# Where the last 64 rows of Wv stand among the first weight loads of a recurrent transformer kernel

## The chip, the cores and the metric

The kernel runs on one core of one Trainium2 chip. The metric is device time in microseconds (us) from one launch, the median of several runs. Everything is bf16 with fp32 sums in PSUM.

## The reference

Two blocks are applied twice, each as `x = x + block(layernorm(x))`, over a sequence of 2048 tokens of width 576. The first block is attention with a recurrent memory: the sequence is cut into 64 segments of 32 tokens, each is preceded by 8 memory tokens, and the first 8 output tokens of a segment are the memory of the next. The second is a gated feed-forward of width 4608.

```python
for s in range(n_seg):
    xs = x[:, s * seg_len:(s + 1) * seg_len, :].copy()
    h = jnp.concatenate([mem, xs], axis=1)
    q = jnp.einsum('btd,dhe->bhte', h, Wq)
    k = jnp.einsum('btd,dhe->bhte', h, Wk)
    v = jnp.einsum('btd,dhe->bhte', h, Wv)
    scores = jnp.einsum('bhqe,bhke->bhqk', q, k) * scale
    scores = jnp.where(mask[None, None], scores, -1000000000.0)
    p = _softmax(scores, axis=-1)
    o = jnp.einsum('bhqk,bhke->bhqe', p, v)
    o = jnp.einsum('bhte,hed->btd', o, Wo)
    mem = o[:, :M, :].copy()
    outs.append(o[:, M:, :])
# feed-forward: silu(x @ w1) * (x @ w3) @ w2
```

There are 32 heads of 128, so Wq, Wk and Wv are 576 x 4096 each and Wo is 4096 x 576.

## The kernel before

The segments are a chain of 72 steps: in step t the first attention block does segment t and the second one segment t - 8, and feed-forward work fills the gaps between. Which matmul comes when on PE is a string of letters (`ORDER`) written out by hand. A planner gives every other engine its order from costs, priorities and buffers. SP issues most transfers, ACT four at the start and one at the end. WARM adds plain matmuls at named places, so that PE has something to do there.

The width of 576 is not a multiple of 128: every weight with 576 rows is four blocks of 128 rows and a tail of 64. The tails of Wq and Wk lie side by side in one buffer, `W[:, 8, :]`, each over 64 partitions, 4096 columns. The tail of Wv is 64 rows of 4096 columns as well, but its buffer, the last 2048 columns of `WV`, spreads it over all 128 partitions: columns are cut into 8 pieces of 512, and piece 2q + r lies in the 64 partitions r of columns 512 q and on (q from 0 to 3, r 0 or 1).

All weights of the attention are loaded in one burst at the start. In the order of the program these are, as the text calls them:

- ACT: the tail of Wk, the first 128 tokens (`XN`), the memory (`XTB`, 8 rows), and the half r = 1 of the Wv tail;
- SP: the tail of Wq, the half r = 0 of the Wv tail, then the first halves of the columns of Wq and Wk (four transfers each of 128 rows, 0.5 MB apiece, `load_qk(0)`), their second halves (`load_qk(1)`), the four blocks of Wv (1 MB apiece, `load_v`), the four parts of Wo by groups of 8 heads (`load_o`), and then the first feed-forward weights.

Each transfer takes one of eight semaphores in turn (`DMAHW0` to `DMAHW7`), and its issue waits until the transfer before it on that semaphore has landed. So at most eight are under way.

On PE the first step is: transposes of the first tokens, warm matmuls that read Wk (three for each block, each waiting for its block), Q and K of the first four quarters of the heads (`QK`, `QKt` is its tail part), one group of scores, 22 warm matmuls, Q and K of the other heads, softmax work between, then V. For t = 0 V begins with its tail (16 matmuls of 64 rows, letters `vx`), followed by the four blocks in turn (64 matmuls, letter `X`), a block for all banks at a time. Then come the product with the probabilities (`PV`) and the output projection by groups of 8 heads (`WO`, 32 matmuls and 8 for its tail columns); group g reads part g of Wo.

Of the kernel before, what the change touches and what calls it, by code (L numbers as in the profile page):

```python
# [9 lines left out]
ACT = mybir.ActivationFunctionType  # L10
# [3 lines left out]
P = 128  # L14
R64 = 64
D = 576
# [10 lines left out]
NG = 4  # L27
# [215 lines left out]
def make_nodes(em, nseg, pools, o=Opt, dma_bw=230e3, load_bw=400e3):  # L243
# [4 lines left out]
    def node(*a, **k):  # L248
        n = Node(*a, **k)
        nodes.append(n)  # L250
        return n
# [5 lines left out]
    kb = lambda rows, cols: rows * cols * 2  # L257
# [9 lines left out]
    def load(name, nbytes, prio, fn, deps=()):  # L267
        return node("DMA", nbytes / load_bw, fn, deps=deps, prio=prio, name=name, lat=2.0)

    node("DMA", 4.0, lambda n: None, prio=-999.0, name="boot")  # L270
    ld_m0 = node("ACT", 0.6, em.load_m0(), prio=-90, name="m0", lat=8.0)
    ld_t = [load("ldt", 1.7 * kb(3 * R64, 4096), -10.0, em.load_tails(0)), node("ACT", 0.6, em.load_tails(1), prio=-120, name="ldt", lat=8.0)]
    node("ACT", 0.6, em.load_tails(2), prio=-80, name="ldt", lat=10.0)
    ld_h = [load("ldqk", kb(512, 4096), half - 9.0, em.load_qk(half)) for half in (0, 1)]
    ld_v = [load("ldv", kb(512, 4096), -7.0, em.load_v())]
    ld_o = [load("ldo", kb(1024, 576), g - 6.0, em.load_o(g)) for g in range(NG)]

    b = banks(1)
# [349 lines left out]
class Emitter:  # L628
# [110 lines left out]
        return f  # L739

    def load_tails(self, what):
        def f(n):
            if what < 2:
                d, wd = (self.dma, self.a.wq) if what == 0 else (self.adma, self.a.wk)
                d(self.T.W[what * R64:(what + 1) * R64, 8, :], wd[4 * P:D, :])
            if what != 1:
                r = what // 2
                (self.adma if r else self.dma)(self.wv(True)[r * R64:(r + 1) * R64, :].rearrange("p (q n) -> p q n", q=NG),
                                               self.a.wv[4 * P:D, :].rearrange("p (q r n) -> r p q n", q=NG, r=2)[r])
        return f  # L750

    def wv(self, tail):
        if tail:
# [2 lines left out]

    def load_v(self):
        def f(n):
            for c in range(4):
                self.dma(self.wv(False)[:, c, :], self.a.wv[c * P:(c + 1) * P, :])  # L760
        return f
# [555 lines left out]
def kernel(  # L1317
# [26 lines left out]
    em = Emitter(nc, tc, T, a, nseg)  # L1344
    pools = dict(POOLS)
    nodes = make_nodes(em, nseg, pools)

    wp = ctx.enter_context(tc.tile_pool(name="wts", bufs=1))
# [97 lines left out]
```

## Time and profile before

| | |
|---|---|
| median of 3 runs | 2624.2 us (2623.95 to 2626.34) |
| profiled execution | 2624.02 us |
| its span, first to last instruction | 2622.2 us |
| PE busy | 98% |
| DVE, ACT, POOL busy | 77%, 48%, 7% |
| bytes moved | 369.58 MB, 141 GB/s over the span |
| first fortieth of the span (65.6 us) | PE 60%, 326 GB/s |
| granted TensorE clock | 0.999 |

The profile is of one execution. All times in it count from the first instruction. A row of a timeline gives start, duration, engine, line, operation and the tiles written and read; lines with "DMA" on SPq or ACTq are issues of transfers, whose duration is the issue alone. "DMA to landing" is the time from issue until the data have arrived. L653, L672 and L675 are the helpers that record every matmul, every transfer of SP and every transfer of ACT, so one goes by tiles.

### The profile page before, as it was taken

What the parts mean: (1) busy time and instruction counts of PE and PEld (TensorE: products, weight loads), DVE (VectorE), ACT (ScalarE), POOL (GpSimd) and SP (SyncE); (2) the same over time, 40 slices, a digit from 0 to 9 for tenths busy, and PEclk for the clock granted to TensorE, in tenths of its full rate; (3) what the DMA queues carried; (4) which work ended last, traced back from release to release, by engine and by line L of the source; (5) the groups of instructions that cost most, each with busy time, mean ns of one, the idle gap of its engine ahead of it and who ended that gap; (6) DMA issues with size and microseconds to landing.
All of it is one profiled execution on the core that took longest, in us unless ns stands there. A gap on an engine that the chain in (4) does not pass through costs nothing.

```text
span 2622.2 us, 131462 instructions
## 1 busy us (share of the span) xinstructions
PE 2567.1 (98%) x58447; PEld 2205.6 (84%) x58498; DVE 2009.5 (77%) x5145; ACT 1266.8 (48%) x3743; POOL 196.1 (7%) x253
## 2 busy tenths in 40 slices
PE   6999999999999999999999999999999999999998
PEld 4788888888888888888888888888888888888887
DVE  4778777787787688777867877786787778777877
ACT  2655453544545354454535445453544545445553
POOL 1100000000001000000000000010000000010000
PEclk9999999999999999999999999999999999999999
DMA  9064746565464656555465655546465554554447
GB/s 326 4 181 126 193 103 154 126 152 136 126 139 115 148 128 153 135 126 141 115 148 128 155 133 127 144 109 151 128 156 132 126 143 112 128 146 129 123 131 258
DMA packets 680217, 369.58 MB, mean 141 GB/s; under 512 B 233592, under 2 KB 669824, under 8 KB 679008
## 3 DMA queue, kind: packets, MB, share of 16 engines
q1 hardware_dynamic: 675968, 353.23, 52.5%
q8 instruction: 457, 7.49, 1.2%
q0 software_dynamic: 3024, 6.93, 0.9%
q10 hardware_dynamic: 656, 1.02, 0.2%
q14 instruction: 112, 0.92, 0.1%
HBM read 304.95 MB, written 2.36 MB: 117 GB/s over the span
## 4 chain that ended last, share of the span: by engine, by line
PE 90%; DMA 4%; DVE 3%; SPq 1%; issue 1%; ACT 1%; ACTq 0%; DVEq 0%
PE bank L653 90%; DMA PTS<-PB 2%; DMA W<-in_B_w_dram 1%; SPq L672 1%; DVE STAT L669 1%; DVE PB L669 1%; DVE SME L669 1%; DMA WV<-in_A_Wv_dram 0%; DVE HTT L669 0%; DMA W<-in_A_Wk_dram 0%; ACT V L666 0%; DVE V L669 0%; PE bank L663 0%; DMA W2C<-in_B_w_dram 0%; ACT HT L666 0%
## 5 line engine op out<-in xcount | busy, mean ns | idle before, releaser
L653 PEld LDWEIGHTS <-W 128*128 128x128 bf16 (+2 forms) x32096 | 1252.3, 100 | 121.3 <-issue 66.1
L653 PE MATMUL bank<-HT,W 128*128 128x80 bf16 (+3 forms) x23040 | 792.9, 197 | 9.6 <-ACT HT L666 5.4
L653 PE MATMUL bank<-XTB,W 128*64 128x256 bf16 (+5 forms) x9056 | 662.5, 264 | 4.5 <-DMA W<-in_B_w_dram 4.2
L666 ACT ACTIVATE QKT<-bank 128x192 bf16<-128x192 f32 (+4 forms) x1674 | 382.2, 312 | 274.5 <-PE bank L653 268.7
L653 PE MATMUL bank<-OT,WO 128*128 128x80 bf16 (+3 forms) x11520 | 411.1, 198 | 1.3 <-issue 1.3
L653 PEld LDWEIGHTS <-WO 128*128 128x128 bf16 (+1 forms) x11520 | 380.4, 102 | 27.6 <-issue 13.4
L666 ACT ACTIVATE V<-bank 64x512 bf16<-64x512 f32 (+1 forms) x589 | 333.0, 585 | 136.7 <-PE bank L653 129.8
L653 PE MATMUL bank<-WV,HT 128*32 128x512 bf16 (+4 forms) x3430 | 355.9, 381 | 6.8 <-issue 4.3
L653 PE MATMUL bank<-W2C,HTT 128*64 128x288 bf16 (+1 forms) x3152 | 322.1, 287 | 0.7 <-DMA W2C<-in_B_w_dram 0.6
L666 ACT ACTIVATE HTT<-bank 128x512 bf16<-128x512 f32 (+1 forms) x324 | 173.1, 550 | 284.0 <-PE bank L653 283.1
L669 DVE SCALAR_TENSOR_TENSOR XR<-bank,XR 128x288 f32<-128x288 f32 x574 | 243.4, 448 | 59.0 <-PE bank L653 53.4
L669 DVE TENSOR_REDUCE STAT<-SME 104x8 f32<-104x320 f32 (+1 forms) x576 | 273.8, 475 | 12.2 <-ACT SME L666 5.0
L669 DVE TENSOR_TENSOR PB<-SME,STAT 40x128 bf16<-40x128 f32 (+4 forms) x912 | 275.1, 336 | 8.1 <-issue 0.2
L653 PEld LDWEIGHTS <-HT 128*32 128x32 bf16 (+4 forms) x3472 | 147.5, 98 | 140.3 <-issue 24.9
L1092 POOL MEMSET PB<- 128x1024 bf16 x142 | 134.8, 951 | 1742.7 <-DMA PTS<-PB 1219.4
L653 PEld LDWEIGHTS <-HTT 128*64 128x64 bf16 (+1 forms) x3232 | 231.4, 105 | 35.7 <-issue 5.6
L669 DVE SCALAR_TENSOR_TENSOR HTT<-HTT,bank 128x512 bf16<-128x512 bf16 (+1 forms) x324 | 200.9, 620 | 69.7 <-ACT HTT L666 65.8
L666 ACT ACTIVATE OT<-bank 128x320 bf16<-128x320 f32 (+1 forms) x389 | 145.1, 402 | 203.8 <-PE bank L653 196.6
L669 DVE TENSOR_TENSOR HTT<-HTT,bank 128x512 bf16<-128x512 bf16 (+1 forms) x324 | 203.5, 628 | 28.0 <-DVE HTT L669 0.9
L666 ACT ACTIVATE SME<-SME 104x320 f32<-104x320 f32 (+1 forms) x288 | 135.0, 469 | 180.9 <-DVE SME L669 179.0
L669 DVE CAST V<-bank 64x512 bf16<-64x512 f32 (+1 forms) x275 | 188.3, 685 | 40.8 <-PE bank L653 36.4
L669 DVE TENSOR_TENSOR SME<-bank,maskb 104x320 f32<-104x320 f32 (+1 forms) x288 | 138.9, 483 | 39.4 <-PE bank L653 36.1
(61 smaller groups left out, 1400.8 us busy)
## 6 DMA issues: line engine op xcount, KB each, us to landing
W<-in_B_w_dram SPq DMA_DIRECT2D x604, 256.0 KB, 3.5
W2C<-in_B_w_dram SPq DMA_DIRECT2D x302, 288.0 KB, 3.5
W<-in_B_w_dram SPq DMA_DIRECT2D x604, 32.0 KB, 3.5
W<-in_B_w_dram SPq DMA_DIRECT2D x8, 1024.0 KB, 13.0
W<-in_A_Wq_dram SPq DMA_DIRECT2D x9, 512.0 KB, 9.9
WO<-in_A_Wo_dram SPq DMA_DIRECT2D x4, 1152.0 KB, 16.8
XR<-in_A_x_dram POOLq DMA_DIRECT2D x16, 288.0 KB, 2.9
WV<-in_B_w_dram SPq DMA_DIRECT2D x4, 1152.0 KB, 12.3
```

Source lines behind the costliest of these rows:

```text
L653: self.ch("PE", self.nc.tensor.matmul(out, lhsT=lhsT, rhs=rhs, start=start, stop=stop, skip_group_check=True, **k))
L666: self.ch("ACT", self.nc.scalar.activation(*a, **k))
L669: self.ch("DVE", getattr(self.nc.vector, fn_)(*a, **k))
L672: self.ch("SP", self.nc.sync.dma_start(out=out, in_=in_))
L1092: return lambda n: self.ch("POOL", self.nc.gpsimd.memset(self.pbt(pb), 0.0))
```

## The change

The two transfers of the Wv tail are gone from the head of ACT's and SP's queues. In their place four stand on SP behind the second halves of Wq and Wk, ahead of the blocks of Wv. Each fills 512 columns of all 128 partitions; its source is a view of Wv with r (2) outermost, then the 64 rows, then 512 columns.

```diff
-    ld_t = [load("ldt", 1.7 * kb(3 * R64, 4096), -10.0, em.load_tails(0)), node("ACT", 0.6, em.load_tails(1), prio=-120, name="ldt", lat=8.0)]
-    node("ACT", 0.6, em.load_tails(2), prio=-80, name="ldt", lat=10.0)
+    ld_t = [load("ldt", 1.7 * kb(2 * R64, 4096), -10.0, em.load_tails(0)), node("ACT", 0.6, em.load_tails(1), prio=-120, name="ldt", lat=8.0)]
     ld_h = [load("ldqk", kb(512, 4096), half - 9.0, em.load_qk(half)) for half in (0, 1)]
-    ld_v = [load("ldv", kb(512, 4096), -7.0, em.load_v())]
+    ld_v = [load("ldv", kb(576, 4096), -7.0, em.load_v())]
...
     def load_tails(self, what):
-        def f(n):
-            if what < 2:
-                d, wd = (self.dma, self.a.wq) if what == 0 else (self.adma, self.a.wk)
-                d(self.T.W[what * R64:(what + 1) * R64, 8, :], wd[4 * P:D, :])
-            if what != 1:
-                r = what // 2
-                (self.adma if r else self.dma)(self.wv(True)[r * R64:(r + 1) * R64, :].rearrange("p (q n) -> p q n", q=NG),
-                                               self.a.wv[4 * P:D, :].rearrange("p (q r n) -> r p q n", q=NG, r=2)[r])
-        return f
+        d, wd = (self.dma, self.a.wq) if what == 0 else (self.adma, self.a.wk)
+        return lambda n: d(self.T.W[what * R64:(what + 1) * R64, 8, :], wd[4 * P:D, :])
...
     def load_v(self):
         def f(n):
+            for q in range(NG):
+                self.dma(self.wv(True)[:, q * 512:(q + 1) * 512], self.a.wv[4 * P:D, q * 1024:(q + 1) * 1024].rearrange("p (r n) -> r p n", r=2))
             for c in range(4):
                 self.dma(self.wv(False)[:, c, :], self.a.wv[c * P:(c + 1) * P, :])
         return f
```

SP at the start of the program, before the change; the brackets name the semaphore of the earlier transfer for whose landing the issue waits:

```order
L672 DMA W<-in_A_Wq_dram 64x4096
L672 DMA WV<-in_A_Wv_dram 64x4x512
L672 DMA W<-in_A_Wq_dram 128x2048 x2
L672 DMA W<-in_A_Wq_dram 128x2048 [waits DMAHW0_49]
L672 DMA W<-in_A_Wq_dram 128x2048 [waits DMAHW1_49]
L672 DMA W<-in_A_Wk_dram 128x2048 [waits DMAHW2_49]
L672 DMA W<-in_A_Wk_dram 128x2048 [waits DMAHW3_49]
L672 DMA W<-in_A_Wk_dram 128x2048 [waits DMAHW4_49]
```

And with the change, at the same place:

```order
L671 DMA W<-in_A_Wq_dram 64x4096
L671 DMA W<-in_A_Wq_dram 128x2048 x4
L671 DMA W<-in_A_Wk_dram 128x2048 [waits DMAHW0_49]
L671 DMA W<-in_A_Wk_dram 128x2048 [waits DMAHW1_49]
L671 DMA W<-in_A_Wk_dram 128x2048 [waits DMAHW2_49]
L671 DMA W<-in_A_Wk_dram 128x2048 [waits DMAHW3_49]
```

The transfer of the Wv tail has left SP's head, and all four blocks of Wq are issued there without a wait. The four blocks of Wk now wait for the tail of Wk, the tail of Wq, the first tokens and the first block of Wq, and no more for the two halves of the Wv tail.

SP further on, with the change, from the last block of Wk's second half to the first blocks of Wv; the first dimension of a row is that of the destination's partitions:

```order
L671 DMA W<-in_A_Wk_dram 128x2048 [waits DMAHW3_49]
L671 DMA WV<-in_A_Wv_dram 128x1x512 [waits DMAHW4_49]
L671 DMA WV<-in_A_Wv_dram 128x1x512 [waits DMAHW5_49]
L671 DMA WV<-in_A_Wv_dram 128x1x512 [waits DMAHW6_49]
L671 DMA WV<-in_A_Wv_dram 128x1x512 [waits DMAHW7_49]
L671 DMA WV<-in_A_Wv_dram 128x4096 [waits DMAHW0_49]
L671 DMA WV<-in_A_Wv_dram 128x4096 [waits DMAHW1_49]
```

Before, the row of the last Wk block is followed at once by those of the Wv blocks. The four tail transfers stand ahead of all of Wv and, with it, of Wo and the feed-forward weights.

PE at the start of V in step 0 (the last warm matmul, and the first of the 16 tail matmuls), before:

```order
L663 MATMUL bank_88<-W,ident 128x512
L653 LDWEIGHTS HT
L653 MATMUL bank_88<-WV,HT 32x512
L653 LDWEIGHTS HT
L653 MATMUL bank_88<-WV,HT 32x512
```

And with the change:

```order
L652 LDWEIGHTS HT
L652 MATMUL bank_88<-WV,HT 32x512 [waits DMAHW4_49]
L652 LDWEIGHTS HT
L652 MATMUL bank_88<-WV,HT 32x512 [waits DMAHW5_49]
L652 LDWEIGHTS HT
L652 MATMUL bank_88<-WV,HT 32x512 [waits DMAHW6_49]
L652 LDWEIGHTS HT
L652 MATMUL bank_88<-WV,HT 32x512 [waits DMAHW7_49]
```

Nothing has moved on PE, but the first four tail matmuls now wait for one of the four transfers each. On PE, DVE, ACT and POOL the order of all operations is as before over the whole program (ACT has one issue less), and so is that of the transfers on SP behind the blocks of Wv.

## The prediction

> **What bounds the kernel now.** I read the page first, then the chain of waits of the first 90 us, then DMA and clock in stretches of 2 us, and last the transfers one by one. The chain over the whole span:
>
> ```profile
> PE 90%; DMA 4%; DVE 3%; SPq 1%; issue 1%; ACT 1%; ACTq 0%; DVEq 0%
> ```
>
> PE carries the kernel. The edit touches only the loads of the first 60 us, and the order of the work on PE, DVE and ACT stays the same, so what it does there is added to, or taken from, the end almost one to one. The chain there begins with the very transfers that are moved:
>
> ```profile
> 2.86 11.15 DMA WV<-in_A_Wv_dram
> 14.02 0.02 issue
> 14.03 8.94 DMA W<-in_A_Wk_dram
> 22.97 0.04 issue
> 23.01 5.11 PE bank L653 x170
> ```
>
> ACT's half of the Wv tail lands at 14.02; only then does SP issue the last block of Wk's first half, which lands at 22.97 and starts Q and K. What limits this stage is DMA, as the stretches show (length; PE, PEld, DVE, ACT, POOL; then granted clock, DMA share, GB/s):
>
> ```profile
> 6.00:8.00 2.00, 0.00 (x0) 0.00 (x0) 1.78 (x5) 0.00 (x0) 0.00 (x0) 1.00 0.98 196
> 8.00:10.00 2.00, 0.00 (x0) 0.00 (x0) 0.45 (x1) 0.00 (x0) 0.00 (x0) 1.00 1.09 295
> 10.00:12.00 2.00, 0.00 (x0) 0.00 (x0) 1.18 (x4) 0.00 (x0) 0.56 (x1) 1.00 1.02 321
> 12.00:14.00 2.00, 0.94 (x10) 0.76 (x11) 1.08 (x5) 0.68 (x1) 0.01 (x1) 1.00 1.06 354
> 18.00:20.00 2.00, 2.00 (x6) 0.67 (x5) 0.00 (x0) 0.00 (x0) 0.00 (x0) 1.00 1.07 406
> 44.00:46.00 2.00, 0.82 (x20) 0.20 (x5) 1.78 (x5) 0.67 (x2) 0.00 (x0) 1.00 1.09 390
> 46.00:48.00 2.00, 1.82 (x36) 1.05 (x39) 0.13 (x1) 0.00 (x0) 0.00 (x0) 1.00 1.08 385
> ```
>
> The engines of DMA are full (share about 1) while the Wv tail is under way, yet move only 196 to 354 GB/s; with nothing but Wq and Wk blocks it is 406, and with Wo, whose rows are 1152 bytes, 385 to 390. From here on a transfer lands when all before it in the queue are through.
>
> **The head of the queue.** Removed: two transfers of 256 KB, 0.52 MB together, ahead of Wk's last block. At 406 GB/s that is 1.3 us, at 196 it is 2.7; I take the mean rate of the three stretches from 8 to 14 us, 323 GB/s, so 1.6 us. Second, a wait goes:
>
> ```profile
> 10.03 4.33 SPq L672 DMA_DIRECT2D W<-in_A_Wk_dram  x4
> 24.27 4.16 SPq L672 DMA_DIRECT2D WV<-in_A_Wv_dram  x4
> 29.38 16.75 SPq L672 DMA_DIRECT2D WO<-in_A_Wo_dram  x4
> ```
> ```profile
> SPq L672 <- DMA WV<-in_A_Wv_dram: 2.7, 1, 2.7
> ```
>
> The four Wv issues wait for the four second-half blocks of Wq in turn, so their spacing is that of landings: 4.16 less an issue of 0.33 is 3.83 for three, 1.28 us a block. The fourth Wk block was issued at 14.03, after 2.7 us of waiting. Had it been issued at once, it could have landed up to 2.7 us sooner; if the queue was long enough to hide that, 0 sooner. I take 1.6, a little over one block's spacing, since the engines were full all the while. Gain at the head: 3.2 us, between 1.3 and 5.4. So Q and K would begin at 19.8. Two more rows matter here, the first tokens on their way into HT, and the landing of Wk's last block (issue near 23.0, then 10.2):
>
> ```profile
> 14.61 0.96 ACT L666 ACTIVATE HT<-bank 128x320 bf16<-128x320 bf16 x4
> ```
> ```profile
> L672 SPq DMA_DIRECT2D W<-in_A_Wk_dram x1: 328/328/328, 23.0 to 23.0; - x1
> DMA to landing us min/median/max: 10.2/10.2/10.2
> ```
>
> The tokens are there by 15.6 and are not late. Wk's last block landed at 33.2 and comes 3.2 us sooner as well, at 30.0, so PE keeps the whole gain until V.
>
> **What the four new transfers cost.** They carry the same 0.52 MB. The question is how many of the 16 DMA engines carry it. The source view has r = 2 outermost, the destination 128 partitions. No transfer before has an outermost step so small, but one is near it: the memory, 8 rows. ACT's queue holds these transfers and no others:
>
> ```profile
> q10 hardware_dynamic: 656, 1.02, 0.2%
> ```
> ```profile
> W<-in_A_Wk_dram ACTq DMA_DIRECT2D x1, 512.0 KB, 7.6
> WV<-in_A_Wv_dram ACTq DMA_DIRECT2D x1, 256.0 KB, 11.2
> XN<-in_A_x_dram ACTq DMA_DIRECT2D x1, 144.0 KB, 8.7
> out_dram<-XN ACTq DMA_DIRECT2D x1, 72.0 KB, 1.6
> XTB<-in_A_mem_dram ACTq DMA_DIRECT2D x1, 9.0 KB
> ```
>
> Their contiguous rows are 64 + 256 + 128 + 128 + 8 = 584. The queue has 656 packets, 72 more: 4 x 16 + 8. So four transfers end with one packet on each of 16 engines, and the one of 8 rows with 8: a transfer seems to be dealt out in equal parts along its outermost step. A number of engines that cuts both sides evenly, 2 of the source and 128 of the destination, is 2. I take that as the likeliest: each transfer of 128 KB runs on two engines, 64 KB on each, and all four on the same two.
>
> [...]
>
> The price: four times 64 KB is 262 KB on each of the two. An engine moves a sixteenth of the stretches' rate. Bounds: with 406 GB/s (25.4 per engine) 10.3 us; with Wo's small rows at 390 (24.4) 10.7; with 1 KB rows beside other loads at 321 (20.1) 13.1; at 196 (12.3) 21.4. These are 1 KB rows beside other loads as in the stretch from 10 to 12, so I take 13.1.
>
> Who waits for that: all that stands behind the tails on SP goes over all engines, thus also over these two, and lands 13.1 - 3.2 = 9.9 us later than before. The landings before, the last block of Wv and the last part of Wo:
>
> ```profile
> L672 SPq DMA_DIRECT2D WV<-in_A_Wv_dram x1: 328/328/328, 28.1 to 28.1; - x1
> DMA to landing us min/median/max: 15.1/15.1/15.1
> ...
> L672 SPq DMA_DIRECT2D WO<-in_A_Wo_dram x1: 2898/2898/2898, 43.2 to 43.2; - x1
> DMA to landing us min/median/max: 11.8/11.8/11.8
> ```
>
> That is 43.2 and 55.0; with the change 53.1 and 64.9. And their readers on PE:
>
> ```profile
> 43.79 0.63 PE L653 MATMUL bank<-WV,HT 64*32 64x512 bf16 x16
> 46.18 3.42 PE L653 MATMUL bank<-WV,HT 128*32 128x512 bf16 x60 [0.90 <-DVE V L669]
> 55.14 3.21 PE L653 MATMUL bank<-OT,WO 128*128 128x40 bf16 x116
> ```
>
> V ended at 49.6 with its last block's matmuls, a quarter of 3.42, 0.86 us. Now that block lands at 53.1 and V ends at 54.0, 4.4 us late. The 116 rows of WO are 32 of group 1, 32 of group 2, 16 for tail columns, 32 of group 3 and 4 more, so group 3 began at about 55.14 + 80/116 x 3.21 = 57.4, 2.4 us behind its weights. With V late it would begin at 61.8, but its weights come at 64.9: 7.5 us late. This is the last wait, and it sets the sum: +7.5. Group 2's part (1152 KB at 390 GB/s) comes 3.0 us sooner and is needed 48 rows, 1.3 us, sooner, so it waits less. The four tail matmuls' own waits (the tails land at about 30.0 + 13.1 = 43.1, PE would be there at 40.6) and those for the first Wv blocks lie inside this.
>
> What comes behind is covered: the next tokens are issued and used here:
>
> ```profile
> 57.95 0.47 SPq L672 DMA_DIRECT2D XN<-in_A_x_dram  x1
> ```
> ```profile
> 74.45 0.74 DVE LNS L669 x2
> ```
>
> They may be some 10 us late, of 16.5 between issue and use, and the use is 7.5 us late itself. The other issues and the planner's changed costs move nothing on any engine: 0.
>
> **The sum.** 2624.02 (span 2622.2 and 1.8 around it) + 7.5 = 2631.5. The median is 0.2 above that execution, so I forecast 2631.7. Bounds by the price: the last wait gives 55.0 + price - 3.2 - 57.4, so +4.7 with 10.3 and +15.8 with 21.4.
>
> **Rivals.** *All 16 engines (ends on the other side).* The source's 2 is no limit if the 128 destination partitions decide. Then the tails take 0.52 MB at 390 GB/s, 1.3 us; Wo's last part lands at 55.0 - 3.2 + 1.3 = 53.1, its reader is there at 54.2 and does not wait, and the gain stands whole: 2621.0. For it: the stretches show that the old tails were slow. Against it: the count of 72. The price from which it turns: the two engines would have to need under 2.4 + 3.2 = 5.6 us, half of the smallest bound. [...]
>
> *The clock falls as well.* PE would be idle for much of 41 to 65 us. The trace has one such place, around 152 us:
>
> ```profile
> 152.00:154.00 2.00, 1.29 (x40) 1.21 (x41) 0.00 (x0) 0.00 (x0) 0.00 (x0) 0.94 0.29 79
> 154.00:156.00 2.00, 2.00 (x13) 1.29 (x14) 1.81 (x4) 0.42 (x1) 0.00 (x0) 0.50 0.00 0
> 156.00:158.00 2.00, 2.00 (x49) 1.91 (x46) 1.04 (x3) 0.05 (x1) 0.00 (x0) 0.71 0.61 158
> ```
>
> After idle time the granted clock was 0.50 and 0.71 for two stretches, 0.06 x 2 + 0.50 x 2 + 0.29 x 2 = 1.7 us of full clock lost. One or two such drops behind the last wait would make it 2633.4 to 2635.1. Against it: most of a drop would lie under the waits for weights.
>
> *The waits are there but smaller.* With the price at its low end it is +4.7, 2628.9, still a loss, but within the bound below.
>
> **How the numbers follow.** A measurement of this kernel can tell about 0.2%, 5.2 us, from no change. Two engines without a drop of the clock: 0.64, of which 0.08 lie under +5.2. With a drop: 0.19, all slower. All 16 engines: 0.13, mostly within the bound at -3.2, 0.03 beyond it if the head gains the full 5.4. The rest, 0.04, is half slower and half faster. Slower: 0.56 + 0.19 + 0.02 = 0.77; same: 0.08 + 0.10 = 0.18; faster: 0.03 + 0.02 = 0.05. The two cases with two engines alone reach from 2628.9 to about 2640; with the unsure gain of the head 2626 to 2641, which holds 8 in 10.
>
> **What would show it.** Right: Q and K begin near 19.8 instead of 23.0; the four tail transfers take some 3 us more each to land; PE waits for DMA into WV and WO between 40 and 65; WO of group 3 begins near 65, and from there all is 7 to 8 us late to the end. DMA moves far below 390 GB/s for some 10 us behind Wk. Wrong: the four tails land within 1.5 us of each other, and PE has no new wait for WV or WO; or the start of Q and K has not moved.

## The result, and the profile after

| | before | after |
|---|---|---|
| median, 9 runs each | 2622.71 us (2617.34 to 2630.14) | 2629.69 us (2627.48 to 2634.42) |
| ratio, with its 95% interval | | 1.0034 [1.0023, 1.0046] |
| profiled execution, its span | 2624.02 us, 2622.2 us | 2629.61 us, 2627.8 us |
| granted TensorE clock | 0.999 | 0.997 |

The change makes the kernel 7.0 us slower by the medians and 8.9 us by the ratio. The forecast was 2631.7 us, 7.5 more than the 2624.2 us of the three runs before.

PE's timeline of the changed kernel shows the head, the tail of Wv, the four blocks of Wv and the output projection. Columns: start, duration, operation, count, and in brackets the idle time before with what ended it.

```profile
18.96 0.81 PE L652 MATMUL bank<-W,ident 128*128 128x512 bf16 x3 [0.29 <-DMA W<-in_A_Wk_dram]
19.60 4.16 PE L652 MATMUL bank<-HT,W 128*128 128x40 bf16 x160
...
30.33 1.80 PE L652 MATMUL bank<-HT,W 128*128 128x40 bf16 x65 [0.93 <-DMA W<-in_A_Wk_dram]
...
39.98 0.39 PE L652 MATMUL bank<-WV,HT 64*32 64x512 bf16 x3
41.13 0.61 PE L652 MATMUL bank<-WV,HT 64*32 64x512 bf16 x13 [0.76 <-DMA WV<-in_A_Wv_dram]
43.50 1.05 PE L652 MATMUL bank<-WV,HT 128*32 128x512 bf16 x16 [1.75 <-DMA WV<-in_A_Wv_dram]
...
51.07 1.57 PE L652 MATMUL bank<-WV,HT 128*32 128x512 bf16 x16 [0.66 <-DMA WV<-in_A_Wv_dram]
...
60.01 1.33 PE L652 MATMUL bank<-OT,WO 128*128 128x40 bf16 x48 [0.96 <-DMA WO<-in_A_Wo_dram]
63.88 1.58 PE L652 MATMUL bank<-OT,WO 128*128 128x40 bf16 x40 [2.54 <-DMA WO<-in_A_Wo_dram]
```

The row at 23.01 before stands here at 18.96: the head is 4.05 us earlier. The rows in brackets further down are new. Before, V and WO waited for no transfer; now the fourth tail transfer holds PE until 41.13, the last block of Wv until 51.07, and the last part of Wo until 63.88. The layer norm of the next tokens began at 74.45 before; its row here, on DVE, begins at 81.2, so the loss there is 6.8 us:

```profile
L668 DVE BATCH_NORM_STATS2 LNS<-XN x2: 434/440/445, 81.2 to 81.6; 128x6 f32<-128x288 bf16 x2
```

Where the gain turned into a loss is seen in what DMA moves from 20 to 60 us, in slices of 1 us. First before:

```profile
GB/s 385 340 397 414 418 406 426 406 410 406 422 430 442 393 426 418 434 401 393 442 390 402 354 385 392 388 380 391 392 406 369 379 388 366 351 351 326 345 224 351
```

Then after, with the busy share of the 16 engines in tenths:

```profile
DMA  9999999952111118897999999989999999999999
GB/s 414 410 401 430 401 401 414 406 194 82 48 48 48 48 65 171 342 371 248 356 368 410 410 393 451 434 346 397 395 401 367 380 391 389 392 389 388 392 385 307
```

From 30 to 34 us only 48 GB/s move. The stretches give the share in hundredths for the same place, and the clock later (length; PE, PEld, DVE, ACT, POOL; granted clock, DMA share, GB/s):

```profile
30.00:32.00 2.00, 1.67 (x65) 1.64 (x65) 0.33 (x1) 0.30 (x1) 0.00 (x0) 1.00 0.14 48
...
46.00:48.00 2.00, 1.88 (x16) 0.62 (x16) 0.00 (x0) 0.00 (x0) 0.00 (x0) 0.50 0.97 372
...
64.00:66.00 2.00, 2.00 (x42) 1.58 (x42) 0.01 (x1) 0.40 (x2) 0.00 (x0) 0.50 0.73 209
66.00:68.00 2.00, 2.00 (x60) 1.68 (x58) 0.68 (x4) 0.50 (x2) 0.00 (x0) 0.50 0.85 245
68.00:70.00 2.00, 2.00 (x67) 1.97 (x66) 0.46 (x2) 0.42 (x3) 0.00 (x0) 0.69 0.07 25
```

A share of 0.14 is a little over two engines of 16 (0.125), and 48 GB/s are 24 for each of two. The single packets in the trace show the same: the 512 packets of 1 KB that make up the tails run from 28.43 to 40.32 us, and their busy time is that of 2.2 engines throughout. A group of 128, one transfer, is through at 31.2, 33.9, 36.6 and 40.3 us. Two of the four transfers had been issued by 25.04, and still no more than two engines worked on them, so all four ran on the same two, one behind the other.

The other fourteen have nothing to do, because SP does not hand out more. The chain of waits runs through SP's issues themselves:

```profile
22.62 2.42 SPq L671
25.04 0.04 issue
25.09 3.88 SPq L671
28.97 0.04 issue
29.01 2.53 SPq L671
31.54 0.04 issue
31.59 3.01 SPq L671
...
50.94 12.90 DMA WO<-in_A_Wo_dram
```

The rows at 22.62, 25.09 and 29.01 are the second to fourth tail transfer, the one at 31.59 is the first block of Wv. The tails' issues take 2.4 to 3.9 us and that of the block 3.0; in swap16 below, at the same place, they take 0.53 to 0.55 and 0.34. What holds them is not shown. A long issue alone is nothing new: the second part of Wo took 8.7 us to issue before as well (from 30.63 on), but DMA moved 393 to 442 GB/s beside it, in the slices from 30 to 40 us. Here the first block of Wv is out only at 34.60, and from there DMA comes back to life: 65, 171 and 342 GB/s in the slices at 34, 35 and 36.

### The profile page after: what moved, and what is told of

Same layout as the page of the kernel before. It is cut to its first block, busy times and chain, and to the rows that moved or that the text cites. A ratio compares the mean times of both kernels' runs of the same rounds, so it can differ in the third digit from the quotient of the medians.

```text
span 2627.8 us, 131514 instructions
## 1 busy us (share of the span) xinstructions
PE 2575.2 (98%) x58498; PEld 2205.1 (84%) x58498; DVE 2008.7 (76%) x5145; ACT 1267.3 (48%) x3743; POOL 196.3 (7%) x253
## 3 DMA queue, kind: packets, MB, share of 16 engines
q1 hardware_dynamic: 676216, 353.49, 52.6%
## 4 chain that ended last, share of the span: by engine, by line
PE 89%; DMA 4%; DVE 3%; SPq 2%; issue 1%; ACT 0%; DVEq 0%; ACTq 0%
PE bank L652 89%; SPq L671 2%; DMA PTS<-PB 2%; DMA W<-in_B_w_dram 1%; DMA W<-in_A_Wq_dram 1%; DVE STAT L668 1%; DVE PB L668 1%; DVE HTT L668 1%; DVE SME L668 1%; DMA WO<-in_A_Wo_dram 0%; DVE V L668 0%; ACT HT L665 0%; DVE XR L668 0%; ACT QKT L665 0%; DVE QKT L668 0%
## 5 line engine op out<-in xcount | busy, mean ns | idle before, releaser
L652 PE MATMUL bank<-WV,HT 128*32 128x512 bf16 (+4 forms) x3472 | 365.8, 384 | 5.6 <-DMA WV<-in_A_Wv_dram 5.2
L668 DVE SCALAR_TENSOR_TENSOR XR<-bank,XR 128x288 f32<-128x288 f32 x574 | 243.1, 448 | 58.4 <-PE bank L652 53.1
```

Of the source, the lines that this page charges most:

```text
L652: self.ch("PE", self.nc.tensor.matmul(out, lhsT=lhsT, rhs=rhs, start=start, stop=stop, skip_group_check=True, **k))
L668: self.ch("DVE", getattr(self.nc.vector, fn_)(*a, **k))
```

## Experiments

The table sets the runs side by side. "Head" is where the first matmul of Q and K has gone (23.66 before, 19.60 with the change), "at LNS" where the row of 74.4 has gone, both in us of one profiled execution. The ratio is to the kernel before, run on the same chip.

| kernel | head | at LNS | ratio, 95% |
|---|---|---|---|
| the change (source's outermost step 2) | -4.1 | +6.8 | 1.0034 [1.0023, 1.0046] |
| outer4 (4) | -3.7 | +4.0 | 1.0011 [1.0001, 1.0020] |
| outer8 (8) | -3.6 | -1.3 | 0.9987 [0.9978, 0.9997] |
| swap16 (64) | -3.2 | -2.8 | 0.9986 [0.9977, 0.9995] |
| form_ahead (2, at the old place) | +7.7 | +6.9 | 1.0032 [1.0017, 1.0048] |
| swap_ahead (64, at the old place) | -1.3 | -1.3 | 1.0001 [0.9990, 1.0012] |
| two_behind (old form, new place) | -3.6 | -0.6 | 0.9995 [0.9987, 1.0004] |
| half_behind (old form, one half moved) | -3.0 | -0.8 | 0.9995 [0.9983, 1.0008] |
| eight_behind (eight of 64 KB) | -3.3 | +1.8 | 1.0010 [0.9999, 1.0020] |
| paired (old form, ACT's half earlier) | -1.7 | -1.2 | 1.0013 [1.0005, 1.0022] |

### swap16: the same four transfers with the rows outermost

```diff
-                self.dma(self.wv(True)[:, q * 512:(q + 1) * 512], self.a.wv[4 * P:D, q * 1024:(q + 1) * 1024].rearrange("p (r n) -> r p n", r=2))
+                self.dma(self.wv(True)[:, q * 512:(q + 1) * 512], self.a.wv[4 * P:D, q * 1024:(q + 1) * 1024].rearrange("p (r n) -> p r n", r=2))
```

> The four transfers of the changed kernel, at the same place, of the same size and into the same 128 partitions x 512 columns; only the two outer steps of the source view are swapped, so that 64 stands outermost in place of 2 (the rows of the tail then lie in other partitions than the matmuls expect). Two engines by the outermost step (my theory): the transfers spread over 16 engines. DMA stays above 350 GB/s between 28 and 36 us where the changed kernel had 48; the four tails are through in about 1.5 us; Q and K begin near 19.6; no wait of PE for WO; from 70 us on everything is 3 to 4 us earlier than in the kernel before, about 0.9985 of its time. Rival, small pieces (128 KB in rows of 1 KB are slow by themselves): as the changed kernel, DMA far below 350 GB/s behind Wk and 6 to 9 us later than before. Rival, the place (anything ahead of Wv's blocks delays V): V's last block 1 us or more later than in the kernel before.

Its stretches behind Wk, which answer to the 48 GB/s of the change:

```profile
28.00:30.00 2.00, 2.00 (x19) 0.84 (x17) 0.43 (x2) 0.00 (x0) 0.00 (x0) 1.00 1.10 385
30.00:32.00 2.00, 1.63 (x63) 1.53 (x61) 0.32 (x1) 0.30 (x1) 0.00 (x0) 1.00 1.06 420
```

And PE where it needs the last block of Wk, and later the last of Wo:

```profile
30.68 1.80 PE L652 MATMUL bank<-HT,W 128*128 128x40 bf16 x65 [0.37 <-DMA W<-in_A_Wk_dram]
...
54.09 1.14 PE L652 MATMUL bank<-OT,WO 128*128 128x40 bf16 x36 [0.26 <-DMA WO<-in_A_Wo_dram]
```

Nothing but the order of the source's steps differs, the bytes and the 1 KB rows are the same, and DMA moves 385 and 420 GB/s; of the waits for Wv and Wo only 0.26 us is left. Most of the gain of the head stays: 2.8 us at LNS, where 3 to 4 were expected, and 2620.21 us where this rival of the prediction had been given 2621.0. This is the run that decides: the order of the steps made the loss.

### outer4 and outer8: the outermost step at 4 and at 8

```diff
-                self.dma(self.wv(True)[:, q * 512:(q + 1) * 512], self.a.wv[4 * P:D, q * 1024:(q + 1) * 1024].rearrange("p (r n) -> r p n", r=2))
+                self.dma(self.wv(True)[:, q * 512:(q + 1) * 512], self.a.wv[4 * P + q % 2 * 32:4 * P + (q % 2 + 1) * 32, q // 2 * 2048:(q // 2 + 1) * 2048].rearrange("p (r n) -> r p n", r=4))
```

Above outer4, and outer8 in the same place:

```diff
+                self.dma(self.wv(True)[:, q * 512:(q + 1) * 512], self.a.wv[4 * P + q * 16:4 * P + (q + 1) * 16, :].rearrange("p (r n) -> r p n", r=8))
```

> The changed kernel with an outermost step of 4 in place of 2 in the source view (four column pieces of 32 rows each per transfer; the same bytes, size and destination, but other rows in each partition than the matmuls expect). Two engines by the outermost step: now four engines, 131 KB on each, 5.4 us at 24 GB/s. A stretch behind Wk with a DMA share near 0.25 and some 96 GB/s, half as long as in the changed kernel; V's last block lands near 44.6, Wo's last part near 56.3, and from 70 us on all is between 2 us earlier and 1 us later than before. Rival, small pieces or the place: as the changed kernel, 6 to 9 us later than before.

> The changed kernel with an outermost step of 8 in the source view (eight column pieces of 16 rows each per transfer; other rows in each partition than the matmuls expect). Eight engines carry 64 KB each, 2.7 us at 24 GB/s, up to 4.6 if they are slowed beside other loads as in outer4 (205 to 265 GB/s from 28 to 36 us). Between swap16 and outer4: from 70 us on 2 us earlier to 2 us later than before. If the count of engines did not matter, it would stand with outer4 or with swap16.

Outer4, two stretches and the last wait for Wo on PE:

```profile
30.00:32.00 2.00, 1.22 (x49) 1.22 (x49) 0.33 (x1) 0.30 (x1) 0.00 (x0) 1.00 0.93 259
32.00:34.00 2.00, 2.00 (x59) 1.74 (x55) 0.93 (x3) 0.74 (x2) 0.00 (x0) 0.65 1.06 265
```
```profile
60.93 1.58 PE L652 MATMUL bank<-OT,WO 128*128 128x40 bf16 x40 [2.45 <-DMA WO<-in_A_Wo_dram]
```

The loss falls with the step, +6.8, +4.0, -1.3 and -2.8 us at LNS for 2, 4, 8 and 64, as the number of engines would have it. Outer8 came out inside its range of -2 to +2. For outer4 the size was missed: a shift of -2 to +1 was expected and +4.0 came. Its tails took 7.7 us by their packets (28.74 to 36.41) where 5.4 was expected: some 95 GB/s from 29 to 31 us, and 53 to 69 behind that, beside the blocks of Wv, when the engines moved only 259 and 265 GB/s at shares of 0.93 and 1.06. The tails stretch into the time of the next transfers and both are slow there; why is not shown.

The packets on the queues can be counted for the engines as well, with each ending taken for one engine, as in the prediction. SP's queue before and after, and SP's in the three others (packets, MB, share of 16 engines):

```profile
q1 hardware_dynamic: 675968, 353.23, 52.5%
```
```profile
q1 hardware_dynamic: 676216, 353.49, 52.6%
```
```profile
q1 hardware_dynamic: 676224, 353.49, 52.4%
```
```profile
q1 hardware_dynamic: 676240, 353.49, 53.0%
```
```profile
q1 hardware_dynamic: 676272, 353.49, 52.9%
```

In this order: before, the change, outer4, outer8, swap16. Each lost SP's half of the tail (256 rows and 16 endings, 272) and won 512 rows and the endings of four transfers. 676216 - 675968 + 272 - 512 = 8 endings, 2 for each transfer; for the others the same sum gives 16, 32 and 64, so 4, 8 and 16 each. So outermost steps of 2, 4, 8 and 64, all into 128 partitions, gave 2, 4, 8 and 16 endings a transfer. The 2 of the change agrees with its share of 0.14, and the 4 of outer4 with the 95 GB/s of its tails, four times 24.

### form_ahead and swap_ahead: both forms at the old place

```diff
+            if what == 0:
+                for q in range(NG):
+                    self.dma(self.wv(True)[:, q * 512:(q + 1) * 512], self.a.wv[4 * P:D, q * 1024:(q + 1) * 1024].rearrange("p (r n) -> r p n", r=2))
```

The four transfers stand in `load_tails(0)`, behind the tail of Wq, and no more in `load_v`. Swap_ahead has `"p (r n) -> p r n"` in the same line.

> The form alone: the four transfers with 2 outermost, but at the head of SP's queue, ahead of Wq and Wk, where the kernel before has its own. Two engines by the outermost step: the two engines are 11 to 13 us behind from the start, so every block of Wq and Wk ends that much later on them; Q and K begin near 30 instead of 23, Wo's last part lands near 65, and from 70 us on all is 7 to 10 us later than before. Rival, the place: with the tails ahead it is as the kernel before, within 1 us. Rival, small pieces: they would delay all 16 engines alike, so no stretch with a DMA share of 0.14.

> The four transfers of swap16 (all 16 engines, all partitions; rows in other partitions than the matmuls expect) at the old place, the head of SP's queue. It parts the move from the form. If the old tails were dear because each wrote only half of the partitions, most of the gain of the head comes from the form: Q and K begin 1.5 to 2.5 us earlier than before, near 21, and from 70 us on all is 1 to 2.5 us earlier. If it is the place, Q and K begin near 23 as before.

The head of form_ahead on PE:

```profile
26.49 4.99 PE L652 MATMUL bank<-W,ident 128*128 128x512 bf16 x12 [14.21 <-DMA W<-in_A_Wk_dram]
```

PE waits 14.2 us for Wk, and nothing later waits for Wv or Wo. DMA has a share of 0.14 and 48 GB/s here too, from 10 to 14 us. The form alone costs about 7 us where it stands ahead (7 to 10 were expected), and about as much net where it stands behind, though it hits quite different readers. With the other form at the same place (swap_ahead) the head is 1.3 us earlier than before, a little less than the 1.5 to 2.5 that were expected if half the partitions were what made the old tails dear. So against the change's +6.8 the place is worth little and the form nearly all: at the new place the two forms differ by 9.6 us at LNS (+6.8 and -2.8), at the old place by 8.1.

### two_behind and half_behind: the old form at the new place

```diff
+            for r in (0, 1):
+                self.dma(self.wv(True)[r * R64:(r + 1) * R64, :].rearrange("p (q n) -> p q n", q=NG),
+                         self.a.wv[4 * P:D, :].rearrange("p (q r n) -> r p q n", q=NG, r=2)[r])
```

These lines stand in `load_v` ahead of the blocks, in place of the four transfers. Half_behind has there r = 1 alone, and r = 0 stays at the head.

> The move alone: the Wv tail goes behind the second halves of Wq and Wk as in the changed kernel, but in the two transfers over 64 partitions that the kernel before has. Two engines by the outermost step: these run on 16 engines, the head keeps its gain of about 4 us (Q and K near 19.6), 0.52 MB take 1.6 to 2.6 us behind Wk, Wo's last part lands near 53, and from 70 us on all is 3 to 4 us earlier than before, about 0.9985. Rival, the place: V and WO wait for their weights and it is 6 to 9 us later than before, as the changed kernel. Rival, small pieces: rows are 1 KB here as well, so as slow as the changed kernel if rows of 1 KB are the cause.

> The kernel before with only ACT's half of the Wv tail moved behind the second halves of Wq and Wk (still 64 partitions, now on SP); SP's half stays at the head. It splits the gain of the head. If the wait of the fourth Wk block for ACT's transfer is most of it, Q and K begin 2.5 us or more earlier than before, near 20.3. If bytes ahead are most of it, half of them are gone and Q and K begin 1 to 2 us earlier, 21 to 22.

Two_behind, DMA behind Wk and the next wait on PE:

```profile
28.00:30.00 2.00, 2.00 (x23) 0.90 (x20) 0.16 (x1) 0.00 (x0) 0.00 (x0) 1.00 1.10 251
30.00:32.00 2.00, 0.03 (x2) 0.00 (x0) 0.00 (x0) 0.00 (x0) 0.00 (x0) 1.00 1.16 226
```
```profile
32.19 1.79 PE L652 MATMUL bank<-HT,W 128*128 128x40 bf16 x65 [2.15 <-DMA W<-in_A_Wk_dram]
```

All engines are busy, at shares of 1.10 and 1.16, and move 251 and 226 GB/s, where swap16 moved 385 and 420 with the same bytes over 128 partitions. Even the end of Wk, which was queued ahead, comes later (32.19 against 30.68 in swap16), and 2.15 us of PE go there. With 0.6 us more for the last part of Wo, this is where the expected gain of 3 to 4 us went; 0.6 is left at LNS. What makes these two transfers slower is not shown: they fill 64 partitions each, and are of 256 KB where those of swap16 are of 128. Half_behind has the same wait of 2.15 us. Its head is 3.0 us earlier with ACT's half alone moved, against 3.6 with both: ACT's half, and what waits for it, is most of the head.

### eight_behind: 64 KB pieces, halves in turn

```diff
-                self.dma(self.wv(True)[:, q * 512:(q + 1) * 512], self.a.wv[4 * P:D, q * 1024:(q + 1) * 1024].rearrange("p (r n) -> r p n", r=2))
+                for r in (0, 1):
+                    self.dma(self.wv(True)[r * R64:(r + 1) * R64, q * 512:(q + 1) * 512], self.a.wv[4 * P:D, (2 * q + r) * 512:(2 * q + r + 1) * 512])
```

> The Wv tail at the new place in eight transfers of 64 KB (64 partitions x 512 columns each), the two halves of the partitions in turn; every row lies where the matmuls expect it. The number of engines follows the outermost step (64): all 16, no stretch with a DMA share of 0.14. If rows of 1 KB or small transfers were the cause, this is at least as slow as the changed kernel: 6 to 9 us later than before from 70 us on. If it is only that all 16 engines crowd into one half of the partitions (as in two_behind, 226 to 278 GB/s from 28 to 34 us), the halves in turn ease it: 300 GB/s or more there, and 1 to 3 us earlier than before from 70 us on.

```profile
30.00:32.00 2.00, 0.31 (x13) 0.21 (x9) 0.00 (x0) 0.00 (x0) 0.00 (x0) 1.00 0.29 74
32.00:34.00 2.00, 2.00 (x76) 1.88 (x73) 0.65 (x2) 0.62 (x3) 0.00 (x0) 0.91 0.60 99
```
```profile
19.34 12.41 DMA W<-in_A_Wk_dram
31.75 0.02 issue
31.77 0.47 SPq L671
32.23 0.04 issue
32.27 0.58 SPq L671
```

Expected was a gain of 1 to 3 us, measured a loss of 1.8 at LNS. The outermost step is 64 here, as in swap16 with its 16 endings, and DMA still runs dry, 74 and 99 GB/s at shares of 0.29 and 0.60. The rows point to another reason. Eight small transfers take up all eight semaphores, and the eighth takes the one of Wk's last block: its issue, at 31.77, waits until that block has landed, at 31.75. The first 1 MB block of Wv stands behind it and is issued at 32.27, where swap16 issues it at 25.59. That this alone empties DMA was not tried apart.

### paired: the old tails side by side

```diff
-    node("ACT", 0.6, em.load_tails(2), prio=-80, name="ldt", lat=10.0)
+    node("ACT", 0.6, em.load_tails(2), prio=-110, name="ldt", lat=10.0)
```

> The kernel before with one priority changed: ACT's half of the Wv tail is issued right behind Wk's tail and ahead of XN, so that the two halves, which write the two halves of the partitions, are on the way at the same time. No byte moves behind Wk and every row stands where the matmuls expect it. Theory (the head's wait is for ACT's half of the Wv tail, whose landing releases SP's issue of Wk's fourth block): that landing comes earlier, the fourth block is issued earlier, and Q and K begin at 20.5 to 21.3 us, 1.7 to 2.7 us earlier than before; XN lands about 1 us later, still ahead of its reader; the shift at 70 us is 1 to 2.5 us earlier, ratio 0.9990 to 0.9996. Rival (the bytes ahead of Wk set the head, not the wait): Q and K begin as before, within 0.5 us, and the ratio is 1.000.

SP's issue of Wk's fourth block stood at 14.03 before, and the block landed 8.94 us later. In paired, Wk's first block and its fourth:

```profile
L672 SPq DMA_DIRECT2D W<-in_A_Wk_dram x1: 328/328/328, 12.1 to 12.1; - x1
...
L672 SPq DMA_DIRECT2D W<-in_A_Wk_dram x1: 432/432/432, 14.1 to 14.1; - x1
DMA to landing us min/median/max: 7.1/7.1/7.1
```
```profile
21.27 0.81 PE L653 MATMUL bank<-W,ident 128*128 128x512 bf16 x3 [0.42 <-DMA W<-in_A_Wk_dram]
```

And the fourth block with the change:

```profile
L671 SPq DMA_DIRECT2D W<-in_A_Wk_dram x1: 328/328/328, 10.0 to 10.0; - x1
DMA to landing us min/median/max: 8.9/8.9/8.9
```

The head came 1.7 us earlier with not a byte moved behind Wk, as the theory said, but not in the way it said. ACT's half does land earlier, at 12.1 instead of 14.0. Yet it is now Wk's first block whose issue waits for it (12.1, and 10.0 before), and the fourth is issued at 14.1, as before. What is shorter is its way from issue to landing, by 1.8 us; why is not shown. With the change it is the reverse: the fourth block is issued 4.0 us earlier and takes as long as before. So the order of the old tails alone moves the head, but that the fourth block's wait is what costs there is not shown.

The time did not follow: 1.0013, where 0.9990 to 0.9996 was expected. The profile of paired, which gives its head, is of the fastest of its twelve runs (2620.39 us; the median is 2624.30). Outer8, swap_ahead and paired all stand at -1.2 to -1.3 at LNS and have ratios of 0.9987, 1.0001 and 1.0013. What happens behind 75 us moves the time by some 3 us either way; which part of it differs is open. Differences of the head below that can't be read from the times, and no version here is shown to beat the kernel before by its head alone. The two with intervals below 1, swap16 and outer8, put the rows of the tail elsewhere and are measurements, not versions to use.

## Why the prediction was right

The sign, the mechanism and the size held: the time came out 2.0 us below the forecast, inside the range; the loss is 7.0 us by the medians, where 7.5 was forecast. Step by step:

- **The gain of the head** was mis-sized: 3.2 us forecast, 4.05 measured, inside its bounds of 1.3 to 5.4. The sum gave 1.6 to the bytes and 1.6 to the wait of Wk's fourth block. That issue came 4.0 us earlier and the landing as much; how much of it is the bytes and how much the wait, no run parts, and paired does not either.
- **Two engines** held: share 0.14, 48 GB/s, and 2 endings a transfer. The source's step limits the number although the destination has 128 partitions: 2, 4 and 8 endings for steps of 2, 4 and 8. That the destination counts too, as the prediction took it, is not shown: no run gives it the smaller step. That all four transfers share the same two engines was taken without a row for it, and agrees with the 2.2 engines that their packets kept busy from 28.43 to 40.32 us.
- **The price** of 13.1 us held as a sum, not in its parts, and so by some luck. By their packets the tails kept the two engines for 11.9 us. By the last part of Wo the price is 12.9: landing at 50.94 + 12.90 = 63.84 where 55.0 stood before, 8.8 later, and 4.05 given up. The rate was put at 20.1 GB/s an engine throughout, from a stretch in which the old tails over 64 partitions were under way; it was 24 while the two ran alone, and 17 to 18 from about 37 us on, beside the blocks of Wv.
- **What the text missed:** that SP itself would be held in its issues, so that fourteen engines stand idle from about 30 to 34.6 us. The prediction reckoned only with the two engines' own backlog. That backlog is 11.9 of the 12.9 us, and from its end at 40.3 on the blocks of Wv are there for PE every 2.5 us (43.50, 45.98, 48.51, 51.07), so the fourteen's idle time seems to have cost little at the last wait. That is argued from these rows; no run parts the two.
- **What would show it:** DMA was far below 390 GB/s (194 and less) for 8 us behind Wk (28 to 36), and between 248 and 371 for 5 more. The tails were through 2.7, 2.7 and 3.7 us apart, as the 3 us apiece had it.
- **The readers** waited as said, a little earlier: last Wv block 51.07 (forecast 53.1), end of V 52.64 (54.0), WO of group 3 at 63.88 (64.9). It began at 57.4 before, so the last wait is worth 6.5 instead of 7.5.
- **From there to the end** 7 to 8 us were forecast; 6.8 at LNS, 5.6 in the spans, 7.0 in the medians.
- **The rival on the clock** came true in its condition, and not in its price: the clock fell to 0.50 from 46 to 52 us and again from 64 to 68. The first drop lies under the waits for weights, as the text argued against it. The second lies behind the last wait, and from there to LNS the loss still grows by 0.3 us only (6.5 to 6.8), where 1.7 was the price of a drop.
- **The rival with all 16 engines** was wrong for this change and nearly right as a sum: swap16 is that case, 2.8 us earlier at LNS where 3.2 was given.

## What to carry to other kernels

Before a load is moved or recut, look at the outermost step of its source as well as at the partitions it fills (251 and 226 GB/s in two_behind, 385 and 420 in swap16): four transfers of 128 KB on two engines cost as much as some 5 MB on sixteen (12.9 us at the 385 to 420 GB/s of swap16), and the transfers behind them on the queue paid, Wo's last part with a landing 8.8 us later. With each ending taken for one engine, the packet count of a queue told the number of engines here, 2, 4, 8 and 16, by the endings over and above the rows. When a load at the head is slow, look also at the order of the issues there: in paired a change of order alone gave 1.7 us of head without moving the load away, though no gain in time.

## What was not expected of the hardware

- Issues were held for 2.5 to 3.0 us, and the whole queue behind them, while fourteen of sixteen DMA engines were idle (the issues at 29.01 and 31.59 of the changed kernel; the share from 30 to 34 us was 0.14).
- All sixteen engines were shown as busy at 226 to 265 GB/s: with transfers over 64 partitions (two_behind, shares 1.10 and 1.16), and with transfers on four engines beside others (outer4, 0.93 and 1.06). The busy share alone did not tell a full DMA from a slow one: 1.10 stood beside 251 GB/s in two_behind and beside 385 in swap16.
- Two engines alone moved 24 GB/s of 1 KB rows each, about a sixteenth of the 385 to 420 GB/s that sixteen moved in swap16 (24.1 to 26.3): each of the two was nearly as fast as each of the sixteen, they are only two.
